# Earlier routes and two sets of early tiles in a sketched-attention and expert kernel

## The chip, the cores and the metric

The kernel runs on one core of one Trainium2 chip. The metric is the time of one execution in device microseconds. The kernel before took 250.34 us, the median of three runs (250.05 to 256.19). The profile shows one execution, of 226.58 us by the same measure, with a span of 224.9 us from its first to its last instruction; all times inside the kernel below are of that span.

The engines have these names in the profile: PE is TensorE (matmuls and transposes), DVE VectorE, ACT ScalarE, POOL GpSimd, and SP SyncE, which does no arithmetic and issues transfers. Each works through its own instructions in order, and semaphores tie them together.

## What is computed

Two blocks follow each other. The first is attention without a softmax: each query and key of 32 numbers becomes 64 products of two sketches, and the sum over a sequence is then a small matrix for each head.

```python
phi(x) = outer(S1 @ x, S2 @ x)            # 8 x 8 = 64 numbers
kv = einsum('bhsf,bhsd->bhfd', phi(k), v); z = sum(phi(k), axis=s)
x = (phi(q) @ kv) / (phi(q) @ z + 1e-6)   # batch 4, heads 4, 1088 tokens, head size 32
```

The result, 4352 tokens of 128 numbers, goes into the second block, a layer of eight experts in which every token goes to one of them:

```python
e = argmax(x @ w_gate); gate = softmax(x @ w_gate)[e]
out = gate * sigmoid(x @ w_output_gate)[e] * (relu(x @ w1[e]) @ w2[e])   # 128 -> 1024 -> 128
```

All numbers are float32 on the chip.

## The kernel before, in words

**Chunks and groups.** The 4352 tokens are 34 chunks of 128. Four chunks make a group, so there are nine groups, the last of two chunks. The arrays lie in memory turned, so that a group of keys or queries is one transfer.

**Attention stages.** Each group of keys goes through ks (sketch on PE), kb (copy on ACT), kp (products on DVE, L362) and kc (sums on PE, L405, which collect the matrix of a batch; a batch ends inside a chunk). cl, gt, gs, gm and gc close a batch and fold the gate weights into its matrix, so that the attention matmul yields the gate logits too. Each group of queries goes through qs, qb, qp (L362), qt and qc (transposes on PE, L416, and their copy on ACT), qa (the attention matmul on PE, L430), qr, qx (L447, L448), ql (L456) and qz (L463). Queries of a batch need that batch closed.

**Routes.** ROUTES (line 42) joins groups into routes. When the logits of a route are there, rc chooses the expert of each token (L488 to L500), rg and rf make the gate factor, rp counts the tokens ahead of each one by two matmuls (L516, L517), rs makes the row numbers, and rd (send, L538) scatters each chunk of the route by an indirect transfer of GpSimd (L544) into the table xs in memory. There, each expert has its own region, filled from its front; a row holds the 128 numbers, the factor, and the token's number. A counter, carry, runs from route to route. After the last route a last scatter (L796) writes padding behind each expert's rows.

**Tiles.** A tile is 128 rows of one expert. Its stages are tx (transpose of the rows, PE, L803), tv (copy, DVE, L808), tu (8 blocks of the first expert matrix, PE, L815), th (relu, ACT, L822), td (the second matrix, PE, L829), ty (factor, ACT, L839) and to (scatter to the output by GpSimd, L844). The rows of a tile are read by rows(t) (L632), and its two halves of weights, 512 KB each, by weights(t, 0) and weights(t, 1) (L639). Both are issued by SP, at an address from a table that DVE makes (eti: experts, bti: first rows). There are three weight buffers (NW = 3). weights(t + 3, 0) stands behind tu(t), weights(t + 3, 1) behind td(t), and each waits until PE has read the buffer that it overwrites. A load is left out when the buffer has that expert already.

**Early tiles.** When a route is counted but not the last, every expert has some rows already, and its full groups of 128 can be taken as tiles at once. With E = 8 experts at most 8 x 127 rows are not in full groups, so after 16 chunks (MARK = 1, the second route) at least NE = 9 tiles are full (line 232). mn counts, mt calls early_tiles (L584) for their table, then issues weights of tiles 0 to 2 and the rows of all nine. After the last route late_tiles (L595) makes the table of the rest, of which there are NT - NE at most.

**Order of the work.** PLAN (line 32) is an order written out by hand: attention, routes, and the first tiles, stage by stage. Stages are emitted in just this order, and every engine gets its part of it in this order. The loads of keys and queries follow it too, as far as their buffers (NK, NV, NQ) have room. After PLAN, step_(t) takes the tiles in a regular way: tx(t + 2), tv(t + 2), tu(t + 1), th(t + 1), td(t), ty(t), to(t). In td(t) (L825), behind the weights, rows(t + NX) is issued; with NX = 5 that is five tiles ahead, and when t + 3 is 8, the rows of tiles 9 and 10 are issued together. Scatters into xs are declared free of each other (group "rows"), and those of routes behind the mark are declared free of the loads of early rows (group "early"), since they touch other rows.

**Rings.** Row buffers (xin) number NE + NX + 2 = 16, output buffers (y) NE + 1 = 10.

Of the kernel before, what the change touches and what calls it, by code (L numbers as in the profile page):

```python
# [13 lines left out]
F32 = mybir.dt.float32  # L14
I32 = mybir.dt.int32
ALU = mybir.AluOpType
# [3 lines left out]
EPS = 1e-6  # L20
GRP = 512
WARM = 6
NK, NV, NQ = 4, 5, 2
TS = 128
NW = 3
NX = 5

PLAN = """
    ks0 kb0 ks1 kp0 kb1 ks2 kp1 kc0 kb2 kc1 kp2 qs0 kc2 ks3 qb0 cl0 qp0 gt0 kb3 kc2 gs0 kp3 bg0 qt0 qs1 qc0 gm0 qb1
    qs2 gc0 qp1 qa0 qb2 qp2 ks4 qr0 qx0 qt1 kb4 ql0 ks5 kp4 qc1 kc3 kb5 qz0 qs3 kp5 kc4 qb3 qa1 cl1 qp3 kc4 qr1 qx1
    gt1 qt3 gs1 ql1 gm1 qz1 qc3 ks6 rc0 gc1 ks8 kb6 qa3 kb8 kp6 rg0 rp0 qr3 qt2 rs0 rf0 qs4 qc2 qx3 rd0 kc5 qb4 ql3
    qp4 kc6 qa2 cl2 qz3 gt2 qr2 kp8 qt4 gs2 qx2 gm2 qc4 qs5 ql2 qz2 gc2 ks7 rc1 qb5 qa4 kb7 qp5 rp1 rg1 kc6 qr4 rs1
    qt5 rf1 mn1 kp7 qs7 qc5 rd1 mt1 qb7 kc7 kc8 qs6 qx4 qb6 ql4 qp6 qa5 cl3 qp7 gt3 qr5 qt6 gs3 qx5 gm3 qc6 qs8 ql5
    qz4 gc3 qt7 qb8 qz5 rc2 qa6 qc7 qa7 qr6 qp8 rg2 qx6 rp2 qr7 ql6 qx7 qt8 ql7 qc8 tx0 rs2 tx1 qa8 tv0 tv1 rf2 tx2
    qr8 tu0 tv2 rd2 qx8 ql8 qz8 tx3 th0 tu1 tv3 qz7 qz6 rc3 tx4 th1 td0 tv4 rg3 rp3 tu2 ty0 rs3 rf3 rc4 td1 th2 rg4
    mn4 tu3 mt4 ty1 rd3 td2 th3 tu4 ty2 rf4 rp4 th4 tx5 rs4 tx6 td3 tv5 tv6 rd4 mp4  # L40
"""
ROUTES = ((0, 1), (2, 3), (4, 5), (6,), (7, 8))
MARK = 1
NOWHERE = 1 << 20


# [5 lines left out]
def kernel(  # L52
# [12 lines left out]
    nc = tc.nc  # L65
# [3 lines left out]
    DM = H * D  # L69
    E = w_d.shape[0]  # L70
# [8 lines left out]
    W = DM + 16  # L79
    CAP = N + TS  # L80
    NT = (N + E * (TS - 1)) // TS
    PR = E * TS // 128

    consts = ctx.enter_context(tc.tile_pool(name="consts", bufs=1))
# [10 lines left out]
    def ring(pool, tag, n, shape):  # L95
        turns[tag] = [pool.tile(shape, F32, tag=f"{tag}{i}", name=f"{tag}{i}") for i in range(n)], [0]
# [89 lines left out]
    def half(a):  # L186
        return slice(a * FC * 128, (a + 1) * FC * 128)
# [21 lines left out]
    ones = consts.tile([128, 128], F32, tag="ones")  # L209
# [15 lines left out]

    routes = [range(groups[r[0]][0], groups[r[-1]][-1] + 1) for r in ROUTES]
    duo = {g: i for i, r in enumerate(ROUTES) for g in r}
    RG = max(len(rs) for rs in routes)

    NE = -(-((routes[MARK][-1] + 1) * 128 - E * (TS - 1)) // TS)
    assert 0 < NE <= NT
    ring(consts, "xsT", 3, [128, TS])
    ring(consts, "hT", 2, [128, FC, TS])
    ring(consts, "y", NE + 1, [TS, DM])
    ring(consts, "xin", NE + NX + 2, [TS, W])
    eps = consts.tile([128, 1], F32, tag="eps")
    nc.gpsimd.memset(eps, EPS)
    fresh = {}  # L240
# [15 lines left out]
    pad = consts.tile([128, PR, W], F32, tag="pad")  # L256
# [19 lines left out]
    stepT = consts.tile([128, NT], F32, tag="stepT")  # L276
# [261 lines left out]
    def send(i, ey, sloti, co):  # L538
        n = len(routes[i])
        x = xts.pop(i)  # L540
        nc.gpsimd.tensor_copy(x.bitcast(I32)[:, :n, DM + 1], ids[:, routes[i][0]:routes[i][-1] + 1])
        nc.gpsimd.tensor_mul(x[:, :n, DM], co[:, :n], ey[:, :n, E + 1])  # L542
        for j in range(n):
            apart("rows", nc.gpsimd.indirect_dma_start(  # L544
                out=xs[:, :], out_offset=bass.IndirectOffsetOnAxis(ap=sloti[:, j:j + 1], axis=0),
                in_=x[:, j], in_offset=None, bounds_check=E * CAP - 1), *(["early"] if i > MARK else []))


    eti = consts.tile([128, NT], I32, tag="eti")
    bti = consts.tile([128, NT], I32, tag="bti")  # L550

    def spread(t, n):
        return t[:, :E].unsqueeze(1).to_broadcast((128, n, E))

    def table(t0, n, ends, jump, first, last=None):


        past = consts.tile([128, n, E], F32, tag=f"past{t0}", name="past")
        et = consts.tile([128, n], F32, tag=f"et{t0}", name="et")
        nc.vector.tensor_tensor(past, step[:, :n].unsqueeze(2).to_broadcast((128, n, E)), spread(ends, n), op=ALU.is_ge)  # L560
        with nc.allow_low_precision("numbers of experts are whole"):
            nc.vector.tensor_reduce(eti[:, t0:t0 + n], past[:, :, :E - 1], axis=AX, op=ALU.add)
        nc.vector.tensor_mul(past, past, spread(jump, n))
        nc.vector.tensor_reduce(et, past[:, :, :E - 1], axis=AX, op=ALU.add)
        if last is None:
            nc.vector.tensor_tensor(bti[:, t0:t0 + n], et, stepT[:, :n], op=ALU.add)
        else:

            nc.vector.scalar_tensor_tensor(out=et, in0=et, scalar=first, in1=stepT[:, :n], op0=ALU.add, op1=ALU.add)
            nc.vector.tensor_scalar(bti[:, t0:t0 + n], et, last, None, op0=ALU.min)  # L570

    NS = N // TS
    more = consts.tile([128, 1], I32, tag="more")
    done = consts.tile([128, E + 1], F32, tag="done")
    nc.vector.memset(done, 0.0)
    early = consts.tile([128, E + 1], F32, tag="early")
    nc.vector.memset(early, 0.0)

    def counted():
        ps = psum.tile([128, E], F32, tag="rt", name="ps_n")  # L580
        nc.tensor.matmul(ps, ones, state["carry"], start=True, stop=True)
        return ps

    def early_tiles(ps):  # L584
        full = consts.tile([128, E], I32, tag="full")
        jump = consts.tile([128, E], F32, tag="jump")
        nc.vector.tensor_tensor(full, ps, ecap, op=ALU.subtract)
        nc.vector.tensor_single_scalar(full, full, TS.bit_length() - 1, op=ALU.logical_shift_right)
        nc.vector.tensor_tensor_scan(done[:, 1:], ones[:, :E], full, 0.0, op0=ALU.mult, op1=ALU.add)
        nc.vector.tensor_scalar_min(done[:, 1:], done[:, 1:], float(NE))  # L590
        nc.vector.tensor_sub(early[:, :E], done[:, 1:], done[:, :E])
        nc.vector.tensor_scalar(jump, early[:, :E], -float(TS), float(CAP), op0=ALU.mult, op1=ALU.add)
        table(0, NE, done[:, 1:], jump, None)

    def late_tiles(ps):  # L595
        num = consts.tile([128, E], F32, tag="num")
# [17 lines left out]
        nc.vector.tensor_tensor_scan(ends, ones[:, :E], nt, 0.0, op0=ALU.mult, op1=ALU.add)  # L614
        nc.vector.tensor_single_scalar(more, ends[:, E - 1:], float(NS - NE), op=ALU.subtract)
        nc.vector.tensor_tensor(jump, early[:, 1:], left, op=ALU.subtract)
# [6 lines left out]
    regs, xin, xTs, hTs = {}, {}, {}, {}  # L623
# [5 lines left out]
    def rows(t):  # L629
        at = value(bti, t, E * CAP - TS)  # L630
        xin[t] = nxt("xin")
        ins = nc.sync.dma_start(xin[t], xs[bass.ds(at, TS), :])  # L632
        if t < NE:
            tc.add_to_no_dep_group("early", ins.ins)

    def weights(t, a):
        if a == 0:
            regs[t] = value(eti, t, E - 1)
        nc.sync.dma_start(wt[t % NW][a].rearrange("p c x -> p (c x)"),  # L639
                          w_d[bass.ds(regs[t], 1), :, half(a)].rearrange("e p x -> p (e x)"),  # L640
                          cond=regs[t] != regs[t - NW] if t >= NW else None)
# [12 lines left out]
    stages, have, did = {}, {}, set()  # L654
    end = [NT]
# [123 lines left out]

    @stage  # L780
    def mt(i):
        if i == MARK:
            early_tiles(have.pop(("mn", i)))
            for t in range(NW):
                weights(t, 0)
                weights(t, 1)
            for t in range(NE):
                rows(t)
        else:
            late_tiles(have.pop(("mn", i)))  # L790

    @stage
    def mp(i):
        pa, pai = have.pop("pai")
        nc.gpsimd.tensor_copy(pai, pa)
        apart("rows", nc.gpsimd.indirect_dma_start(  # L796
            out=xs[:, :], out_offset=bass.IndirectOffsetOnAxis(ap=pai[:, :1], axis=0),
            in_=pad.rearrange("p a b -> p (a b)"), in_offset=None), "early")

    @stage  # L800
    def tx(t):
# [22 lines left out]
    @stage  # L824
    def td(t):  # L825
        hT = have.pop(("th", t))
        ps = have["td", t] = nxt("kvz").rearrange("p a x -> p (a x)")[:, :DM]
        for c in range(FC):
            nc.tensor.matmul(ps, hT[:, c], wt[t % NW][1][:, c], start=(c == 0), stop=(c == FC - 1))  # L829
        if t + NW < end[0]:  # L830
            weights(t + NW, 1)
        if t + NW >= NE - 1:
            for n in range(NE if t + NW == NE - 1 else t + NX, min(t + NX + 1, end[0])):
                rows(n)

    @stage
    def ty(t):
# [85 lines left out]
```

## Time and profile before

| what | value |
|---|---|
| time, median of three runs | 250.34 us |
| span of the profiled execution | 224.9 us |
| mean granted clock of PE | 0.958 |
| PE busy, DVE, ACT, POOL | 200.6, 69.3, 74.0, 78.8 us |
| bytes moved, mean rate | 49.10 MB, 218 GB/s |
| scatters L544, first and last start | 35.0 and 90.6 us |
| first tile half (L815), start in the timeline | 65.1 us |
| last second half (L829), start | 213.2 us |

The page has several parts. The slices divide the span into 40 equal pieces of 5.6 us and give the busy share of each engine in tenths; PEclk is the clock that PE was granted, in tenths of full speed. The waits list who waited for whom, in us in total, times, and longest. The chain is followed back from the last instruction, at each step to what released it. The timeline gives instructions in order of time: start, duration, engine, line, operation, tiles, count, and in square brackets the idle time ahead of it and what ended it. "DMA to landing" is the time from the issue of a transfer to its completion.

### The profile page before, as it was taken

The numbers are of one execution on the slowest core, as the hardware profiler recorded it, in microseconds if no ns is written. First come the engines' busy times: TensorE is split into PE (matmuls) and PEld (weight loads), VectorE is DVE, ScalarE is ACT, GpSimd is POOL, SyncE is SP. The second block draws the span as 40 slices with busy tenths as digits, with TensorE's granted clock in tenths as the row PEclk, the third lists the DMA queues.
The fourth block names the chain that finished last, engine by engine and source line by source line (L and its number), as shares of the span: only waits on it lengthen the run. The fifth ranks groups of instructions, "written<-read, shape, count | busy, mean of one in ns | idle before, by whom it ended". The sixth has DMA issues, their size and how long they took to land.

```text
span 224.9 us, 6588 instructions
## 1 busy us (share of the span) xinstructions
PE 200.6 (89%) x2458; PEld 194.9 (87%) x2458; DVE 69.3 (31%) x221; ACT 74.0 (33%) x140; POOL 78.8 (35%) x130
## 2 busy tenths in 40 slices
PE   7899999999489999907999999999999999999720
PEld 6889999998379999907999999999999999999720
DVE  4557889999645670000000010101010101010000
ACT  2123343425204343400434343433434343434300
POOL 3700006777037747771131313132222223131310
PEclk9999999999958999995999999999999999999995
DMA  5866512349636989966898789989984686883100
GB/s 160 315 193 225 155 50 77 115 117 357 247 94 175 319 294 282 312 254 197 251 315 322 227 237 319 313 314 312 330 311 143 207 263 189 269 292 114 38 30 1
DMA packets 21634, 49.10 MB, mean 218 GB/s; under 512 B 3466, under 2 KB 9100, under 8 KB 21600
## 3 DMA queue, kind: packets, MB, share of 16 engines
q1 hardware_dynamic: 19024, 43.31, 60.2%
q0 software_dynamic: 2416, 5.33, 6.3%
q8 instruction: 21, 0.34, 0.7%
q14 instruction: 13, 0.11, 0.2%
q10 hardware_dynamic: 160, 0.01, 0.0%
HBM read 51.17 MB, written 5.52 MB: 252 GB/s over the span
## 4 chain that ended last, share of the span: by engine, by line
PE 56%; DMA 22%; issue 9%; POOL 7%; DVE 1%; SPq 0%; POOLq 0%; ACT 0%
PE w L815 22%; PE kvz L829 18%; DMA out_dram<-y,xin 12%; POOL xs L544 7%; PE t L346 5%; DMA xs<-pad,pai 4%; PE w L430 2%; PE kvz L405 2%; DMA xs<-x,sloti 2%; DMA wt<-in_w_dram 2%; DMA xin<-xs 2%; PE t L803 2%; PE w L322 2%; PE w L416 1%; DVE kp L362 1%
## 5 line engine op out<-in xcount | busy, mean ns | idle before, releaser
L815 PE MATMUL w<-xsT,wt 128*128 128x128 f32 x592 | 76.0, 284 | 0.0
L829 PE MATMUL kvz<-wt,hT 128*128 128x128 f32 x592 | 72.5, 276 | 1.5 <-SPq L875 1.5
L815 PEld LDWEIGHTS w<-xsT,wt 128*128 128x128 f32 x592 | 72.8, 201 | 0.0
L829 PEld LDWEIGHTS kvz<-wt,hT 128*128 128x128 f32 x592 | 69.5, 193 | 1.7 <-issue 1.7
L844 POOL DMA_INDIRECT out_dram<-y,xin x37 | 35.9, 970 | 88.1 <-DMA wt<-in_w_dram 46.4
L822 ACT ACTIVATE hT<-w 128x1024 f32<-128x1024 f32 x37 | 37.9, 1023 | 69.2 <-PE w L815 69.2
L808 DVE COPY xsT<-t 128x128 f32<-128x128 f32 x38 | 11.0, 291 | 121.9 <-PE t L803 121.9
L544 POOL DMA_INDIRECT xs<-x,sloti x34 | 33.7, 990 | 12.2 <-issue 8.8
L839 ACT ACTIVATE y<-kvz,xin 128x128 f32<-128x128 f32 x37 | 13.6, 367 | 28.6 <-PE kvz L829 28.6
L803 PE MATMUL t<-ident,xin 128*128 128x128 f32 x38 | 11.0, 295 | 10.3 <-DMA xin<-xs 10.3
L803 PEld LDWEIGHTS t<-ident,xin 128*128 128x128 f32 x38 | 5.6, 150 | 11.1 <-DMA xin<-xs 10.9
L430 PE MATMUL w<-kz,qpT 128*64 128x98 f32 x272 | 13.8, 256 | 0.4 <-ACT b_sb L354 0.4
L430 PEld LDWEIGHTS w<-kz,qpT 128*64 128x64 f32 x272 | 12.4, 142 | 0.9 <-ACT b_sb L354 0.5
L542 POOL TENSOR_TENSOR x<-co,ey 128x8 f32<-128x8 f32 (+2 forms) x5 | 1.1, 223 | 33.5 <-DVE rc L447 23.7
L422 ACT COPY qpT<-w 128x1024 f32<-128x1024 f32 (+1 forms) x9 | 8.7, 965 | 9.9 <-PE w L416 9.9
L362 DVE TENSOR_TENSOR qp<-t,b_sb 128x1024 f32<-128x1024 f32 (+1 forms) x9 | 10.4, 1160 | 3.0 <-ACT b_sb L354 2.8
L362 DVE TENSOR_TENSOR kp<-t,b_sb 128x1024 f32<-128x1024 f32 (+1 forms) x9 | 10.4, 1160 | 2.9 <-PE kvz L405 1.8
L405 PE MATMUL kvz<-vt,kp 128*64 128x65 f32 (+1 forms) x288 | 10.5, 223 | 0.0
L346 PE MATMUL t<-Sb,kT 128*64 128x64 f32 x272 | 9.8, 224 | 0.8 <-DVE kp L362 0.5
L354 ACT COPY b_sb<-t 128x128 f32<-128x128 f32 (+1 forms) x18 | 4.7, 259 | 16.4 <-PE t L346 16.1
L346 PEld LDWEIGHTS t<-Sb,kT 128*64 128x64 f32 x272 | 8.7, 138 | 1.6 <-DVE kp L362 0.6
L405 PEld LDWEIGHTS kvz<-vt,kp 128*64 128x64 f32 (+1 forms) x288 | 9.4, 137 | 0.5 <-issue 0.2
(130 smaller groups left out, 120.8 us busy)
## 6 DMA issues: line engine op xcount, KB each, us to landing
wt<-in_w_dram SPq DMA_DIRECT2D x79, 512.0 KB
xin<-xs SPq DMA_DIRECT2D x41, 72.0 KB
vt<-in_v_dram SPq DMA_DIRECT2D x8, 260.0 KB
kT<-in_k_dram SPq DMA_DIRECT2D x8, 256.0 KB
qT<-in_q_dram SPq DMA_DIRECT2D x8, 256.0 KB
out_dram<-y,xin POOLq DMA_INDIRECT x37, 4.7
xs<-x,sloti POOLq DMA_INDIRECT x34, 4.4
vt<-in_v_dram SPq DMA_DIRECT2D x1, 130.0 KB
```

The source lines that it names most:

```text
L346: nc.tensor.matmul(ps[64 * t:64 * (t + 1), j * H:(j + 1) * H], src[:, j * 128 + 64 * t:j * 128 + 64 * (t + 1)], Sb[i], start=i == 0 and j ...
L362: nc.vector.tensor_mul(res[:, :n], bview(av, [list(av.ap[1]), list(av.ap[2]), [0, r]]), bview(bv, [list(bv.ap[1]), [0, r], list(bv.ap[2])]))
L405: nc.tensor.matmul(acc[b][64 * h:64 * (h + 1), s], kp[p0:p0 + np_, j * H + 2 * s + h].rearrange("s i j -> s (i j)"), vt[p0:p0 + np_, j, s] ...
L430: nc.tensor.matmul(ps[64 * t:64 * (t + 1), 2 * j + s, :VG], qpT[:, 2 * j + s, 64 * t:64 * (t + 1)], kz[(c * 128 + 64 * t) // S][:, s], sta ...
L544: apart("rows", nc.gpsimd.indirect_dma_start(out=xs[:, :], out_offset=bass.IndirectOffsetOnAxis(ap=sloti[:, j:j + 1], axis=0), in_=x[:, j] ...
L803: nc.tensor.transpose(have["tx", t], xin[t][:, :DM], ident)
L808: nc.vector.tensor_copy(have["tv", t], have.pop(("tx", t)))
L815: nc.tensor.matmul(ps[:, c], wt[t % NW][0][:, c], xT, start=True, stop=True)
L822: nc.scalar.activation(have["th", t], have.pop(("tu", t)), ACTF.Relu)
L829: nc.tensor.matmul(ps, hT[:, c], wt[t % NW][1][:, c], start=(c == 0), stop=(c == FC - 1))
L839: nc.scalar.activation(have["ty", t], have.pop(("td", t)), ACTF.Copy, scale=xin[t][:, DM:DM + 1])
L844: apart("out", nc.gpsimd.indirect_dma_start(out=out, out_offset=bass.IndirectOffsetOnAxis(ap=x.bitcast(I32)[:, DM + 1:DM + 2], axis=0), in ...
```

## The change

The routes become 4, 8, 8, 8 and 6 chunks, and there are two marks in place of one: tiles 0 to 4 are full behind 12 chunks (the second route), tiles 5 to 12 behind 20 chunks (the third). early_tiles runs once at each mark and takes the full groups that are new since the mark before. The aim is to have rows for the first tiles sooner, and more of them ahead of the late rows, which wait for the last route and the padding. Scatters are declared free of the loads of the early tiles of every mark that lies before them.

PLAN is written anew: first queries come ahead of later keys, and some transposes of tiles stand further ahead. Query buffers become three, NX becomes 4, the ring of row buffers 20 and that of output buffers 14. At the first mark the rows of tiles 0 to 4 are issued, each behind its weights; all other rows, t + NX from tile 5 on, are issued one by one in td(t).

```diff
-NK, NV, NQ = 4, 5, 2
+NK, NV, NQ = 4, 5, 3
-NX = 5
+NX = 4
-ROUTES = ((0, 1), (2, 3), (4, 5), (6,), (7, 8))
-MARK = 1
+ROUTES = ((0,), (1, 2), (3, 4), (5, 6), (7, 8))
+MARKS = (1, 2)
-    NE = -(-((routes[MARK][-1] + 1) * 128 - E * (TS - 1)) // TS)
+    NES = [-(-((routes[m][-1] + 1) * 128 - E * (TS - 1)) // TS) for m in MARKS]
+    NE = NES[-1]
-    ring(consts, "y", NE + 1, [TS, DM])
-    ring(consts, "xin", NE + NX + 2, [TS, W])
+    ring(consts, "y", 14, [TS, DM])
+    ring(consts, "xin", 20, [TS, W])
 ...
-                in_=x[:, j], in_offset=None, bounds_check=E * CAP - 1), *(["early"] if i > MARK else []))
+                in_=x[:, j], in_offset=None, bounds_check=E * CAP - 1), *(f"early{k}" for k, m in enumerate(MARKS) if i > m))
 ...
-    def early_tiles(ps):
+    def early_tiles(k, ps):
+        t0, t1 = ([0] + NES)[k:k + 2]
+        was, now = earlies[k:k + 2]
 ...
+        nc.vector.tensor_tensor(new, full, was[:, :E], op=ALU.subtract)
+        nc.vector.tensor_tensor_scan(ends[:, 1:], ones[:, :E], new, 0.0, op0=ALU.mult, op1=ALU.add)
+        nc.vector.tensor_scalar_min(ends[:, 1:], ends[:, 1:], float(t1 - t0))
+        nc.vector.tensor_sub(new, ends[:, 1:], ends[:, :E])
+        nc.vector.tensor_add(now[:, :E], was[:, :E], new)
 ...
+        table(t0, t1 - t0, ends[:, 1:], jump, first)
 ...
-        if t < NE:
-            tc.add_to_no_dep_group("early", ins.ins)
+        for k, n in enumerate(NES):
+            if t < n:
+                tc.add_to_no_dep_group(f"early{k}", ins.ins)
 ...
-        if i == MARK:
-            early_tiles(have.pop(("mn", i)))
-            for t in range(NW):
-                weights(t, 0)
-                weights(t, 1)
-            for t in range(NE):
+        if i in MARKS:
+            early_tiles(MARKS.index(i), have.pop(("mn", i)))
+        if i == MARKS[0]:
+            for t in range(NES[0]):
+                if t < NW:
+                    weights(t, 0)
+                    weights(t, 1)
                 rows(t)
 ...
-        if t + NW >= NE - 1:
-            for n in range(NE if t + NW == NE - 1 else t + NX, min(t + NX + 1, end[0])):
-                rows(n)
+        if NES[0] <= t + NX < end[0]:
+            rows(t + NX)
```

The new PLAN, in the part that matters for the first tiles (route 3 is sent by rd3, route 4 by rd4):

```
tx0 qr7 qa5 tv0 qx7 ql7 mn2 tx1 qr5 tx2 tv1 tu0 qx5 ql5 tv2 tx3 qz7 th0 tu1 tv3 mt2 td0 th1 tu2 qz5 ty0 rc3 td1
th2 qz8 rg3 to0 rp3 ty1 tx4 rs3 tu3 to1 tv4 rc4 td2 th3 rf3 rg4 tu4 rd3 ty2 rf4 td3 th4 rp4 ty3 tx5 tx6 tv5 td4
rs4 tv6 tu5 ty4 tx7 th5 tx8 tv7 tu6 tv8 td5 th6 to4 tx9 ty5 tu7 tv9 rd4 td6 th7 tx10 ty6 mn4 tu8 mt4 td7 th8
tx11 ty7 tu9 tv11 tv10 to6 td8 th9 mp4
```

More of the change, by code (lines that the diff above doesn't have):

```diff
@@ L22 @@
 WARM = 6
-NK, NV, NQ = 4, 5, 2
+NK, NV, NQ = 4, 5, 3
 TS = 128
 NW = 3
-NX = 5
+NX = 4
 PLAN = """
[L33 to L40, printed above, removed]
-"""
-ROUTES = ((0, 1), (2, 3), (4, 5), (6,), (7, 8))
-MARK = 1
+    ks0 kb0 ks1 kp0 kb1 ks2 kp1 kc0 kb2 qs0 kp2 kc1 qb0 qp0 ks3 kc2 ks4 kb3 cl0 bg0 kp3 gt0 kb4 qt0 gs0 qs1 qc0 gm0
+    qb1 kc2 gc0 qp1 qa0 kp4 qt1 qr0 qx0 qs2 qc1 ql0 ks5 qz0 qb2 rc0 kc3 kb5 kc4 qa1 qp2 rg0 cl1 rp0 qr1 kp5 qt2 ks6
+    rs0 qc2 qx1 gt1 qs3 ql1 gs1 kb6 qz1 gm1 qb3 rf0 kc4 gc1 qp3 rd0 qa2 kp6 qt3 qr2 qx2 ks7 qc3 ql2 kc5 qz2 kb7 rc1
+    kc6 qa3 cl2 rp1 rg1 kp7 kc6 qr3 ks8 rs1 kc7 kb8 rf1 gt2 kp8 rd1 qs4 gs2 qx3 gm2 qb4 ql3 kc8 gc2 qp4 qs8 mn1 qb8
+    cl3 qt4 qp8 mt1 qt8 qc4 qs6 qc8 qa4 qb6 qp6 gt3 qr4 qs7 gs3 qx4 gm3 qb7 qt6 ql4 gc3 qp7 qa8 qc6 qs5 qz4 qr8 qz3
+    qt7 qb5 qx8 ql8 qp5 qc7 qa6 rc2 qt5 qr6 qc5 qx6 rp2 rg2 ql6 rs2 qa7 rf2 qz6 rd2 tx0 qr7 qa5 tv0 qx7 ql7 mn2 tx1
+    qr5 tx2 tv1 tu0 qx5 ql5 tv2 tx3 qz7 th0 tu1 tv3 mt2 td0 th1 tu2 qz5 ty0 rc3 td1 th2 qz8 rg3 to0 rp3 ty1 tx4 rs3
+    tu3 to1 tv4 rc4 td2 th3 rf3 rg4 tu4 rd3 ty2 rf4 td3 th4 rp4 ty3 tx5 tx6 tv5 td4 rs4 tv6 tu5 ty4 tx7 th5 tx8 tv7
+    tu6 tv8 td5 th6 to4 tx9 ty5 tu7 tv9 rd4 td6 th7 tx10 ty6 mn4 tu8 mt4 td7 th8 tx11 ty7 tu9 tv11 tv10 to6 td8 th9
+    mp4
+"""
+ROUTES = ((0,), (1, 2), (3, 4), (5, 6), (7, 8))
+MARKS = (1, 2)
 NOWHERE = 1 << 20
@@ L228 @@
     RG = max(len(rs) for rs in routes)
-    NE = -(-((routes[MARK][-1] + 1) * 128 - E * (TS - 1)) // TS)
-    assert 0 < NE <= NT
+    NES = [-(-((routes[m][-1] + 1) * 128 - E * (TS - 1)) // TS) for m in MARKS]
+    NE = NES[-1]
+    assert 0 < NES[0] and NE <= NT
     ring(consts, "xsT", 3, [128, TS])
     ring(consts, "hT", 2, [128, FC, TS])
-    ring(consts, "y", NE + 1, [TS, DM])
-    ring(consts, "xin", NE + NX + 2, [TS, W])
+    ring(consts, "y", 14, [TS, DM])
+    ring(consts, "xin", 20, [TS, W])
     eps = consts.tile([128, 1], F32, tag="eps")
@@ L565, in table @@
         if last is None:
-            nc.vector.tensor_tensor(bti[:, t0:t0 + n], et, stepT[:, :n], op=ALU.add)
+            nc.vector.scalar_tensor_tensor(out=bti[:, t0:t0 + n], in0=et, scalar=first, in1=stepT[:, :n],
+                                           op0=ALU.add, op1=ALU.add)
         else:
@@ L573 @@
     more = consts.tile([128, 1], I32, tag="more")
[L574 to L577, printed above, removed]
+    earlies = [consts.tile([128, E + 1], F32, tag=f"early{k}", name=f"early{k}") for k in range(len(MARKS) + 1)]
+    for x in earlies:
+        nc.gpsimd.memset(x, 0.0)
+    early = earlies[-1]
     def counted():
@@ L582, in counted @@
         return ps
-    def early_tiles(ps):
-        full = consts.tile([128, E], I32, tag="full")
-        jump = consts.tile([128, E], F32, tag="jump")
+    def early_tiles(k, ps):
+        t0, t1 = ([0] + NES)[k:k + 2]
+        was, now = earlies[k:k + 2]
+        full = consts.tile([128, E], I32, tag=f"full{k}", name="full")
+        new = consts.tile([128, E], F32, tag=f"new{k}", name="new")
+        ends = consts.tile([128, E + 1], F32, tag=f"ends{k}", name="ends")
+        jump = consts.tile([128, E], F32, tag=f"jump{k}", name="jump")
+        first = consts.tile([128, 1], F32, tag=f"first{k}", name="first")
         nc.vector.tensor_tensor(full, ps, ecap, op=ALU.subtract)
+        nc.vector.memset(ends[:, :1], 0.0)
         nc.vector.tensor_single_scalar(full, full, TS.bit_length() - 1, op=ALU.logical_shift_right)
[L589 to L593, printed above, removed]
+        nc.vector.tensor_tensor(new, full, was[:, :E], op=ALU.subtract)
[3 more added lines that the diff above has]
+        nc.vector.tensor_add(now[:, :E], was[:, :E], new)
+        nc.vector.tensor_tensor(jump, was[:, 1:], now[:, :E], op=ALU.subtract)
+        nc.vector.tensor_scalar(jump, jump, float(TS), float(CAP), op0=ALU.mult, op1=ALU.add)
+        nc.vector.tensor_scalar_mul(first, was[:, :1], float(TS))
+        table(t0, t1 - t0, ends[:, 1:], jump, first)
     def late_tiles(ps):
@@ L781, in mt @@
     def mt(i):
-        if i == MARK:
-            early_tiles(have.pop(("mn", i)))
-            for t in range(NW):
-                weights(t, 0)
-                weights(t, 1)
-            for t in range(NE):
+        if i in MARKS:
[5 more added lines that the diff above has]
+                    weights(t, 1)
                 rows(t)
-        else:
+        elif i not in MARKS:
             late_tiles(have.pop(("mn", i)))
@@ L797, in mp @@
             out=xs[:, :], out_offset=bass.IndirectOffsetOnAxis(ap=pai[:, :1], axis=0),
-            in_=pad.rearrange("p a b -> p (a b)"), in_offset=None), "early")
+            in_=pad.rearrange("p a b -> p (a b)"), in_offset=None), *(f"early{k}" for k in range(len(MARKS))))
     @stage
```

## The prediction

> **What bounds the kernel now.** I read the page first (busy shares and slices), then TensorE's waits, the chain that ended last, and the order of time around the two holes. TensorE (PE) is busy 89% of the span; the slices show where it is not: slices 10 and 11, and 17 and 18 (counted from 0).
>
> ```profile
> PE 200.6 (89%) x2458; PEld 194.9 (87%) x2458; DVE 69.3 (31%) x221; ACT 74.0 (33%) x140; POOL 78.8 (35%) x130
> PE   7899999999489999907999999999999999999720
> PEclk9999999999958999995999999999999999999995
> ```
>
> PE's waits say what the holes are: the transposes of token rows (L803) stand for rows read back from the table in memory.
>
> ```profile
> PE t L803 <- DMA xin<-xs: 10.3, 3, 6.8
> PE kvz L829 <- SPq L875: 1.5, 1, 1.5
> ```
>
> The chain (start, us, what) gives the way into each: the last scatter of the marked route lands at 60.15 and its rows are read; later the pad scatter lands at 100.7, then the first late rows.
>
> ```profile
> 54.87 5.26 DMA xs<-x,sloti
> ...
> 60.99 1.90 DMA xin<-xs
> ...
> 92.06 8.63 DMA xs<-pad,pai
> 100.71 1.89 DMA xin<-xs
> ```
>
> PE's timeline after the second hole shows a second price: the first two halves of a tile take 3.62 and 2.24 us where 1.95 is usual, because the clock was granted at half.
>
> ```profile
> 102.64 0.48 PE L803 MATMUL t<-ident,xin 128*128 128x128 f32 x1 [6.80 <-DMA xin<-xs]
> 102.91 3.62 PE L815 MATMUL w<-xsT,wt 128*128 128x128 f32 x16
> 106.33 2.24 PE L829 MATMUL kvz<-wt,hT 128*128 128x128 f32 x16
> 108.41 0.27 PE L803 MATMUL t<-ident,xin 128*128 128x128 f32 x1
> 108.52 1.95 PE L815 MATMUL w<-xsT,wt 128*128 128x128 f32 x16
> ```
>
> Elsewhere PE runs one tile per 3.68 us without a wait (starts of L803 3.68 apart). This stretch of the timeline shows the order SyncE (SP) keeps: a tile's second half ends near 138.0, SP at once issues the weights into the freed buffer, and 0.9 us later the rows of a later tile.
>
> ```profile
> 137.87 0.27 PE L803 MATMUL t<-ident,xin 128*128 128x128 f32 x1
> ...
> 138.06 0.33 SPq L639 DMA_DIRECT2D wt<-in_w_dram  x1
> ...
> 138.97 0.33 SPq L632 DMA_DIRECT2D xin<-xs  x1
> ...
> 141.55 0.27 PE L803 MATMUL t<-ident,xin 128*128 128x128 f32 x1
> ...
> 145.23 0.27 PE L803 MATMUL t<-ident,xin 128*128 128x128 f32 x1
> ```
>
> Rows issued at 138.97 are those of the transpose at 145.23 (NX = 5): a lead of 6.3 us. What they need, by the tile's own view:
>
> ```profile
> DMA to landing us min/median/max: 2.2/4.7/5.6
> ```
>
> So this prefetch has 0.7 us to spare at its worst. By windows the landing is 2.3 with no weights ahead of it (at 100.7), and 3.8 to 5.6 behind a loaded weight half.
>
> **What the Trainium skill says.** "TensorE: Matmul & The Clock Gate", section "Why this matters for your kernels": no idle gaps over about 3 us, or the clock falls back. The trace agrees: after the 2.93 us hole (with 0.53 on each side) and after the 6.80 us hole the granted clock was 0.5 for a time. Same page, "Step-by-step: what each phase is for": matmuls stay in program order, so a transpose whose rows are missing holds everything behind it; the 6.8 us hole is one such. "DMA: Bandwidth & Descriptors", "Anatomy of one DMA": a fixed 2.0 us for each transfer, and semaphores are waited for at the issuing sequencer; the trace has 2.2 as its least landing, and SP's queue standing 7.7 us for the pad.
>
> **Part by part.** *Removed: the two holes.* First: 0.53 + 2.93 + 0.53 = 4.0 idle, and cold excess: chain pieces of L815 3.41 and 2.06 against 1.79, plus some 0.2 at L430 and the transposes, 2.1. Second: 6.8 idle and (3.41 - 1.79) + (2.04 - 1.79) + 0.2 = 2.1. Together 15.0. Rows of tiles 0 to 4 now need 12 chunks: their scatters end a route sooner, and the late rows have four more tiles ahead of them (4 x 3.68 = 14.7 us against a hole of 6.8). I take PE's first tile half at 65.3 - 4.0 = 61.3.
>
> *Attention reordered.* The same products, transposes and matmuls; DVE and PE were both nearly full up to 59 us (DVE 9.4 of 10 us in 50 to 60). The second early_tiles and five more small operations in each: 16 x 0.2 + 5 x 0.2 = 4.2 us of DVE, of which about one lies before the first tile and three beside the tile stage, where DVE is idle most of the time. Fewer L-sums, logits and route work before the first tile give about 2 back. Zero, with plus or minus 2 for the range.
>
> *Weights.* The routing worked out from the inputs gives 37 tiles in both kernels; a tile reloads its buffer unless the tile three before has the same expert, 32 loads before and 34 after. Two more megabytes beside PE work: zero.
>
> *NX 5 to 4, rows issued one by one.* Before, rows 0 to 8 are issued together. Now only 0 to 4 are; rows t + 4 are issued in td(t), behind the weights that wait for td(t). In the built order of instructions the next transposes stand like this:
>
> - Tile 6: rows leave after td2, transpose after tu4, td3 and a placement (4.2 us later). Need 1.0 + 4.7 = 5.7: wait 1.3 (bounds 0 to 1.5).
> - Tile 7: here a new wait comes in. In the built program this load waits for the last scatter of the fourth route (chunks 20 to 27): those scatters were declared free of the early loads, but the load, which now comes later in the program, is not free of them. Placement 3 ends near 61.3 + 5 x 1.79 + 0.5 = 70.7; slots 0.44, a copy 0.2, the choice for six chunks 1.75 and factor 0.57 on DVE follow (73.6); first scatter 0.95 later (as 64.31 to 65.26), seven more at 1.28 (83.5), landing 4.4 (median of xs): 87.9. The rows then land in 2.3 with an empty queue: 90.3. PE is at this transpose after eleven halves: 61.3 + 19.7 + 1.9 + 1.3 = 84.2. Wait 6.1 (bounds 3 to 8). Queued behind it on SP: weights of tile 7 and rows 8; on PE everything.
> - Tile 8: rows issued at about 89.4, landing 3.8: 93.2, PE there at 90.4: 2.8 (1.8 to 3.7).
> - Tiles 9, 10, 11: the transpose stands directly behind td5, td6, td7, whose end releases the weights ahead of the rows. Wait = 1.0 from the end of td to the row issue + landing. I take 3.8, the least landing measured behind a loaded half, as the queue is emptier than before: 4.8 x 3 = 14.4 (3.3 x 3 = 9.9 to 5.7 x 3 = 17.1). Tile 10's wait for the fifth route's scatters is over by then.
> - From tile 12 on the lead is one step less the issue: 2.7 us against 3.8. A wait lengthens the lead of the next, so per tile s = 1.0 + 3.8 - 3.68 - s, s = 0.56. For 23 of 25 tiles a load stands ahead (worked out from the inputs): 12.9 (landing 2.7: 0; 4.7: 23). Pad and late rows are in time, since PE comes later.
>
> *Clock.* Four holes of 2.8 to 6.1 us, shaped like the two that went cold: three drops at 2.1, 6.3 (0 to four full ones, 13.6).
>
> Sum: 1.3 + 6.1 + 2.8 + 14.4 + 12.9 + 6.3 = 43.8 added, 15.0 removed: +28.8. Span 224.9 + 28.8 = 253.7; time 250.34 + 28.8 = 279.1 (the timed runs lie 23.8 above the profiled 226.58; I carry this over).
>
> **Rivals.** *A, the holes close and the rows are in time:* 250.34 - 15.0 = 235.3. For it: the scatters do get earlier, and PE is the bound. Against it: tiles 9 to 11 have a negative lead in the order of instructions; no landing in the trace is under 2.2. *B, waits at their least:* 0 + 3 + 1.8 + 9.9 + 0 = 14.7 against 15.0: 250.0, no change. For it: landings of 2.3 exist where weights are not reloaded. Against it: nearly all tiles reload. *C, the DMA engines stay as full as in steady state (0.9 busy) and the clock stays cold through tiles 7 to 11:* 1.5 + 8 + 3.7 + 17.1 + 13.6 + 23 + 2 for a late first tile = 68.9 - 15.0: 304.2. For it: landings of 4.8 to 5.6 were usual between 130 and 160 us, with all weights reloaded. Against it: longer steps thin out the traffic.
>
> **How the numbers follow.** Main case 0.72, A 0.06, B 0.08, C 0.14. Time 279.1. Range 256 to 300: A and B lie below, a part of C above. Faster 0.06, within 2% 0.07, slower 0.87 (B split over the bound).
>
> **What would show it.** PE's waits with L821 (the same transpose) on xin as the longest by far, near 37 us over some 28 waits; SP's queue waiting once on xs for several us near 80; holes directly after the second halves of tiles 5, 6, 7; a step of about 4.2 in place of 3.68 later; the clock at half near 85 to 120; and the first tile near 61 with no hole at tile 13. Wrong if steps stay at 3.68 (landings under 2.7), or if transposes of tiles 9 to 11 don't wait.

## The result, and the profile after

The changed kernel takes 295.12 us (median of four runs, 293.9 to 296.65), beside 251.59 for the kernel before (250.05 to 256.19): a ratio of 1.176, 95% interval 1.163 to 1.188. It is slower by 43.5 us, where 28.8 were forecast. The time lies in the forecast range.

One thing is needed to read the numbers below: the kernel before takes 253.8 us on one of four chips that the later runs met and 225 us on the three others, and the profile that the prediction was read from (span 224.9) is of the shorter kind, while the time on record is of the longer. So each time below stands beside that of the kernel before on the same chip. Each chip was met on one occasion only; whether the chip or the occasion decides is open, and "kind of chip" says no more than which of the two times the kernel before takes there.

From the page of the changed kernel, from the runs on record (span 294.5 us): busy time of TensorE (PE), its 40 slices and the granted clock. Then PE's longest wait: us in total, times, longest.

```profile
PE 223.2 (76%) x2460; PEld 210.5 (71%) x2460; DVE 72.0 (24%) x240; ACT 73.7 (25%) x140; POOL 79.3 (27%) x133
PE   7799988398739953584488798877978798879840
PEclk9999998579988995756879989999979979999995
```

```profile
PE t L821 <- DMA xin<-xs: 41.8, 23, 5.4
```

The slices hardly reach 9 after the twentieth, and one wait stands for it: the transpose of token rows (L821, L803 before) waits for rows read back, 41.8 us in 23 times where the profile of the kernel before had 10.3 in three. Of the 41.8 us, tiles 6 to 11 have 22.4 and the later ones 19.4.

This profile is not of the same kind of chip as the profile before. The same program on a chip where the kernel before takes 225.28 us took 277.51 (ratio 1.232, 1.225 to 1.238), with a span of 275.3 us. That trace can be laid beside the one of before line by line, and all that follows on single waits is from it. Its slices and clock (PE busy 215.8 us in all), and PE's longest wait:

```profile
PE   7889999983998835728599669888979898879930
PEclk9999999999599768786689999999999999999995
```

```profile
PE t L821 <- DMA xin<-xs: 43.2, 27, 5.2
```

The timeline of PE at the first tiles (start, us, what, and in brackets the idle time ahead of it). Before, the first tile half (L815, now L833) stood here:

```profile
65.11 3.62 PE L815 MATMUL w<-xsT,wt 128*128 128x128 f32 x16
```

Now:

```profile
61.44 0.33 PE L821 MATMUL t<-ident,xin 128*128 128x128 f32 x1
64.11 0.33 PE L821 MATMUL t<-ident,xin 128*128 128x128 f32 x1 [0.52 <-DMA xin<-xs]
68.30 0.45 PE L821 MATMUL t<-ident,xin 128*128 128x128 f32 x1 [3.86 <-DMA xin<-xs]
68.54 3.64 PE L833 MATMUL w<-xsT,wt 128*128 128x128 f32 x16
```

The hole ahead of the tiles is still there, 0.52 + 3.86 us, and the first tile half begins 3.4 us later than before, not 4.0 sooner. The chain of waits (start, us, what) says why:

```profile
51.34 4.68 DMA xs<-x,sloti
56.04 0.33 SPq L647
...
56.88 1.04 SPq L655
...
58.96 0.33 SPq L647
...
59.79 0.33 SPq L655
...
61.19 6.98 DMA xin<-xs
```

SyncE (SP) issues weights (L655) and rows (L647) by turns. The rows of tile 0 wait for the last scatter of their routes (landed at 56.02), and the weights of tiles 1 and 2, which need no scatter, stand behind them in SP's queue; the rows of tiles 1 to 4 stand behind those. The last link, the landing of rows behind these weights, lasts 6.98 us, where the least landing of rows in this trace is 2.2. On the longer kind of chip the hole does not appear: there the first tile half begins at 76.71, and no transpose of tiles 0 to 3 waits for rows.

Tiles 9 and 10, in the timeline of PE of the same trace (at tile 11 the same: 4.44 us of waiting, then a half of 3.62):

```profile
111.89 0.45 PE L821 MATMUL t<-ident,xin 128*128 128x128 f32 x1 [4.81 <-DMA xin<-xs]
112.13 3.46 PE L833 MATMUL w<-xsT,wt 128*128 128x128 f32 x16
115.43 1.95 PE L847 MATMUL kvz<-wt,hT 128*128 128x128 f32 x16
122.55 0.45 PE L821 MATMUL t<-ident,xin 128*128 128x128 f32 x1 [5.17 <-DMA xin<-xs]
123.08 3.76 PE L833 MATMUL w<-xsT,wt 128*128 128x128 f32 x16
```

Each transpose comes straight after a second half (L847), whose end lets the weights and then its rows go; after each of these three holes the matmuls run at half clock (granted 0.50; 3.46 to 3.76 us instead of 1.95). And the steady stage, in PE's timeline:

```profile
182.28 0.33 PE L821 MATMUL t<-ident,xin 128*128 128x128 f32 x1 [0.99 <-DMA xin<-xs]
...
184.24 1.95 PE L847 MATMUL kvz<-wt,hT 128*128 128x128 f32 x16
...
186.54 0.33 PE L821 MATMUL t<-ident,xin 128*128 128x128 f32 x1 [0.35 <-DMA xin<-xs]
...
191.34 0.33 PE L821 MATMUL t<-ident,xin 128*128 128x128 f32 x1 [0.90 <-DMA xin<-xs]
```

Transposes are 4.26 and 4.80 us apart instead of 3.68; from tile 12 on, 25 steps (144.89 to 258.09), the mean step is 4.53.

### The profile page after: what moved, and what is told of

It reads as the page before. It is cut to its first block, busy times and chain, and to the rows that moved or that the text cites. A ratio compares the mean times of both kernels' runs of the same rounds, so it can differ in the third digit from the quotient of the medians.

```text
span 294.5 us, 6603 instructions
## 1 busy us (share of the span) xinstructions
PE 223.2 (76%) x2460; PEld 210.5 (71%) x2460; DVE 72.0 (24%) x240; ACT 73.7 (25%) x140; POOL 79.3 (27%) x133
## 4 chain that ended last, share of the span: by engine, by line
issue 32%; PE 27%; DMA 17%; POOL 8%; another core or an unknown queue 7%; DVE 3%; POOLq 1%; ACT 1%; SPq 1%; DVEq 0%
DMA out_dram<-y,xin 11%; POOL out_dram L861 7%; PE t L349 6%; PE w L833 5%; PE kvz L847 4%; PE kvz L408 4%; PE w L433 3%; DMA xin<-xs 3%; DMA wt<-in_w_dram 3%; PE w L419 2%; PE w L325 1%; DVE qp L365 1%; POOL xs L547 1%; DMA xs<-x,sloti 1%
## 5 line engine op out<-in xcount | busy, mean ns | idle before, releaser
L833 PE MATMUL w<-xsT,wt 128*128 128x128 f32 x592 | 82.5, 299 | 0.9 <-issue 0.9
L847 PE MATMUL kvz<-wt,hT 128*128 128x128 f32 x592 | 77.1, 286 | 5.9 <-ACT hT L840 4.5
L833 PEld LDWEIGHTS w<-xsT,wt 128*128 128x128 f32 x592 | 78.8, 214 | 1.1 <-issue 1.1
L847 PEld LDWEIGHTS kvz<-wt,hT 128*128 128x128 f32 x592 | 74.4, 204 | 6.3 <-ACT hT L840 4.7
L821 PE MATMUL t<-ident,xin 128*128 128x128 f32 x38 | 12.3, 328 | 42.7 <-DMA xin<-xs 41.8
L821 PEld LDWEIGHTS t<-ident,xin 128*128 128x128 f32 x38 | 5.7, 151 | 47.4 <-DMA xin<-xs 28.7
L419 PE MATMUL w<-ident,qp 128*128 128x128 f32 x68 | 11.2, 307 | 4.9 <-DVE qp L365 4.7
L349 PE MATMUL t<-Sb,kT 128*64 128x64 f32 x272 | 10.9, 225 | 3.7 <-issue 2.7
L419 PEld LDWEIGHTS w<-ident,qp 128*128 128x128 f32 x68 | 8.3, 155 | 6.5 <-DVE qp L365 5.1
L349 PE MATMUL t<-Sb,qT 128*64 128x64 f32 x272 | 11.5, 236 | 1.1 <-issue 1.1
L349 PEld LDWEIGHTS t<-Sb,qT 128*64 128x64 f32 x272 | 10.0, 148 | 2.8 <-issue 2.7
```

The source lines that it names most:

```text
L349: nc.tensor.matmul(ps[64 * t:64 * (t + 1), j * H:(j + 1) * H], src[:, j * 128 + 64 * t:j * 128 + 64 * (t + 1)], Sb[i], start=i == 0 and j ...
L419: nc.tensor.transpose(ps[:, 2 * j + s], qp[:, j * H + 2 * s:j * H + 2 * s + 2].rearrange("p h i j -> p (h i j)"), ident)
L821: nc.tensor.transpose(have["tx", t], xin[t][:, :DM], ident)
L833: nc.tensor.matmul(ps[:, c], wt[t % NW][0][:, c], xT, start=True, stop=True)
```

## The experiments

*The kernel before, unchanged,* to see what its longer executions look like.

> The kernel before, unchanged. It is run again because its profile (226.6 us) and its timed runs (250 to 256) lie 24 us apart, while the changed kernel's profile (296.3) and timed runs agree. If the 24 us are stretches in which TensorE and those that wait for it stand while GpSimd issues scatters (seen in the changed kernel at 49 to 57 and 78 to 86 us), a profile near 250 shows such stretches before 95 us and the same tile stage after it. If they are spread over the whole span (a slower clock, slower transfers), the tile step after 105 us is longer than 3.68. Time: 250 either way.

253.31 us beside 253.81 (ratio 1.000, 0.998 to 1.003), span 251.2. From PE's waits and timeline:

```profile
PE t L803 <- DMA xin<-xs: 1.0, 1, 1.0
```

```profile
82.21 1.95 PE L815 MATMUL w<-xsT,wt 128*128 128x128 f32 x16
```

Its waits for rows are 1.0 us in all, not 10.3: PE loses the time elsewhere, 17.1 us of it before the first tile half (82.21 against 65.11), and the tile stage after it steps by 3.68 again. So on this chip nearly nothing of the waits for rows that the prediction took off was there to be taken.

*The changed kernel with only the row lead put back.*

```
-NX = 4
+NX = 5
```

> The changed kernel with NX = 5: rows of every tile from 5 on are issued one tile sooner, nothing else. Theory 1 (rows come too late for their transposes, 22.4 us at tiles 6 to 11, 19.4 later, 13.5 of cold clock): most of these 55 us go, 236 to 250 us, steps of 3.68. Theory 2 (the new order of attention and routes is what costs: the first tile came at 76.7 and not at 61): 280 to 295. Theory 3 (the DMA engines are too full, two more weight loads and more traffic at once): the waits turn from xin to wt, 275 to 295.

256.69 us beside 253.81 (1.010, 1.006 to 1.014). From the waits of PE:

```profile
PE t L821 <- DMA xin<-xs: 4.9, 2, 3.4
PE w L419 <- DVE qp L365: 4.8, 1, 4.8
```

One step of lead takes 36.9 of the 41.8 us of waiting away, and 38.4 us of time: against 295.12 on record, and against 295.13 on the same chip for the kernel of the next experiment but one, which keeps the shorter lead. The expectation that most of the waiting goes came true; its 236 to 250 us did not. What is left of the change gained nothing here.

*The kernel before with only the row lead taken.*

```
-NX = 5
+NX = 4
```

> The kernel before with NX = 4, nothing else: the nine early rows are still issued together, only the rows of later tiles come one tile later. Theory 1: waits at the transposes of tiles 10 on, some 0.8 us a tile as in the changed kernel (19.4 over 25 tiles) and a few cold stretches: 265 to 278. Theories 2 and 3: 248 to 253.

279.95 us (1.101, 1.090 to 1.112), just above the 265 to 278 expected. From PE's waits:

```profile
PE t L803 <- DMA xin<-xs: 22.1, 15, 2.7
```

The shorter lead alone, with the old routes and order, costs 26 us. The rest of the 41 I put down to the early tiles, argued and not tried: the kernel before issues rows 0 to 8 together, so no transpose meets its rows' issue there.

*The changed kernel with the early rows also free of later scatters,* which takes away SP's wait ahead of tile 7.

```
+            for k, m in enumerate(MARKS):
+                if i > m:
+                    tc.add_to_no_dep_group(f"late{k}", ins.ins)
 ...
+            tc.declare_no_dep(ins.ins, group=f"late{k}", reason="the rows are distinct")
```

> The changed kernel, NX = 4 kept, with the loads of early rows declared free of the scatters of routes behind their mark, so that tile 7's rows don't wait for the fourth route nor tile 10's for the fifth. Theory 1: SyncE's wait of 5.7 us on xs goes, the transposes of tiles 7 and 8 wait less, those of 9 to 11 as before: 287 to 293. Theory 2: 294 to 296, no change.

295.13 us, where 287 to 293 were expected if that wait costs time: no gain against the 295.12 on record. From the waits of PE:

```profile
PE t L828 <- DMA xin<-xs: 41.8, 24, 5.6
```

The sum is that of the changed kernel to the tenth, in one wait more. Tile 7 waited 3.62 us in the profile on record and now doesn't wait at all; tiles 8, 9 and 10 wait longer by 1.5, 1.2 and 0.8. So what tile 7 saved, the next ones paid, and SP's wait for the scatters did not set the time.

*Do the scatters hold TensorE?* In the longer executions PE stands while GpSimd issues scatters (last section). Two kernels replace them by plain transfers to fixed rows, in the kernel before; one does so in the changed kernel. They leave out the placing of rows by expert, so their tiles hold other tokens; the scatters of padding and of results stay.

```
-            apart("rows", nc.gpsimd.indirect_dma_start(
-                out=xs[:, :], out_offset=bass.IndirectOffsetOnAxis(ap=sloti[:, j:j + 1], axis=0), ...
+                e, k = FIXED[c]
+                ins = nc.gpsimd.dma_start(xs[e * CAP + k * TS:e * CAP + (k + 1) * TS, :], x[:, j] ...)
```

> The kernel before, in which GpSimd writes each chunk's 128 rows to 128 fixed neighbouring rows of xs with a plain transfer, in place of the indirect scatter of line 544 (left out: the placing by expert, so the tiles hold other tokens; three more transfers fill the places that the chunks leave, so the tile count and every other instruction stay). Theory S, the indirect scatters hold TensorE while GpSimd issues them: without them the time falls from 253 to 224-238 us, since the profile of before that stood at 226.6 us had none of this standing. Theory S', whatever transfer GpSimd issues holds TensorE: 246-254. Theory N, the standing has another cause and only lies beside the scatters: 249-255, and matmuls in groups of 4 to 6 behind waits marked issue near 38 and 60 us all the same.

> As the kernel with plain transfers from GpSimd, but SyncE issues them, so GpSimd issues no transfer before the tiles (left out: the placing of rows by expert, as there). Theories S and S' (GpSimd's issuing holds TensorE): 224-236 us, and the holes of about 10 us at the first tiles' transposes come back, since the attention half ends some 20 us sooner. Theory N: 249-255.

> The changed kernel with the same edit: SyncE writes fixed rows with plain transfers in place of the indirect scatters (left out: the placing of rows by expert). If the holding by the scatters is what my sum missed, this kernel lands where the sum put the changed one: 268-282 us against 295. If the missing 15 us lie elsewhere (larger waits for rows, a colder clock), it stays at 290-297.

These three met a chip where the kernel before took 225.3 us. There the plain transfers from GpSimd gave 223.93 (0.995, 0.988 to 1.002), those from SyncE 228.3 (1.011, 1.004 to 1.018): no standing to take away, so these two do not tell the theories apart. The changed kernel with plain transfers took 272.03, with 45.3 us of waits for rows. That it lands inside 268 to 282 is no proof of the expectation's reason: beside 225.3 it is 46.7 slower. Most of the loss is there without the scatters of rows (with them it is 52.2 beside such a kernel before, as the next experiment shows), so the missing microseconds of my sum had to be looked for in the tiles. The kernel before with SyncE's transfers, on another chip:

> The kernel before with plain transfers of fixed rows from SyncE in place of the indirect scatters (left out: the placing of rows by expert), once more. If the kernel before takes 253 us here, theory S (the scatters hold TensorE): 226-236 and no matmuls in groups of 4 to 6 behind waits marked issue at 38 and 60 us; theory N (another cause): 250-257 with these groups. If the kernel before takes 225 us: 227-229 as in the last comparison, no news.

227.94 beside 225.28 (1.012, 1.007 to 1.018): no standing here either, and no news.

*The changed kernel itself on the shorter kind of chip.*

> The changed kernel once more, beside the kernel before. If the kernel before takes 225 us here as in the last comparison: the sum of the prediction (+28.8) gives 254; theory A, it held but for the holes that are missing in longer executions: 252-258; theory B, the waits for rows and the colder clock are larger than the sum had them, whatever the standing at the scatters does: 266-273 (as with plain transfers, 272), with some 40-45 us of waits for rows. If the kernel before takes 253 us: 294-297 as before, no news.

277.51 beside 225.28. Theory A (252 to 258) is out: not the missing holes alone, but the sum's own terms were too small. 277.5 overshoots theory B's 273 too; its 40 to 45 us of waits for rows came true (43.2).

*Weights ahead of rows at the first mark.*

```
-            for t in range(NES[0]):
-                if t < NW:
-                    weights(t, 0)
-                    weights(t, 1)
-                rows(t)
+            for t in range(NW):
+                weights(t, 0)
+                weights(t, 1)
+            for t in range(NES[0]):
+                rows(t)
```

> The changed kernel with one line group moved: at the first mark all six weight loads are issued before the five row loads, as the kernel before does, in place of weights and rows by turns. Theory H (the rows of tile 0 wait for the scatters of the second route, and the weights and rows of tiles 1 and 2 queue behind them, which is why the hole ahead of the first tile half stayed): the transposes of tiles 1 and 2 wait under 1 us instead of 0.5 and 3.9, the first tile half comes 3.5-5 us sooner, and the time falls by 4-7 us: 270-274 beside 277.5 where the kernel before takes 225 us, or 289-293 beside 295 where it takes 253. Rival (rows come late by the scatters' own landing, not by the queue): no change, 276-279 or 294-297.

272.73 us beside 225.06 (1.207, 1.197 to 1.217). PE's timeline at the first tiles:

```profile
62.34 0.33 PE L821 MATMUL t<-ident,xin 128*128 128x128 f32 x1 [1.49 <-DMA xin<-xs]
...
64.60 1.95 PE L833 MATMUL w<-xsT,wt 128*128 128x128 f32 x16
```

The first tile half begins 3.9 us sooner and at full clock, and the time falls by 4.8 us from the 277.51 of another chip of this kind. Theory H holds, though 1.49 us of waiting stay, more than the "under 1" expected: the last scatter lands at 57.12, and the rows take 5.16 us behind six halves of weights. Not all that is gained lasts: the small matmuls that count the fifth route come 6.7 us sooner (81.30 instead of 88.02), the last second half only 4.1, as tile 6 now waits longer.

*Rows further ahead,* first with the later rows six ahead, then with the weights in front and the later rows five ahead. Both also put the scatter of padding ahead of second half 7.

```
-        if NES[0] <= t + NX < end[0]:
-            rows(t + NX)
+        for n in range(NES[0], end[0]):
+            if n not in asked and n <= t + (NXE if n < NE else NX):
+                asked.add(n)
+                rows(n)
```

> The changed kernel with rows issued further ahead, at no other cost: 8 tiles ahead for the 13 early tiles, 6 for the later ones (NX = 6), and the pad's scatter moved ahead of second half 7. Theory 1, the issue of rows is what costs: the waits for rows of 4.9 us that NX = 5 left go, with about 1 us of clock: 247-251 us, just under the kernel before (253). Rival: the waits for rows are gone at NX = 5 but for a little, and what is left is held by the attention half: 253-257.

> The changed kernel with the rows of the 13 early tiles issued up to 8 tiles ahead, later ones 5 (NX = 5), weights first at the first mark, the pad's scatter ahead of second half 7. Expected from the trace with NX = 6 (227.9 us beside 225.3): minus the 5.0 us wait for weights behind the rows of tile 13 and about 3 us of cold clock after it, minus 4-6 us at the first tiles: 214-220 us beside 225 for the kernel before, or 243-249 beside 253. Rival: the attention half or another wait fills what is freed: 224-228, or 252-256.

The first (NX = 6, NXE = 8) took 227.92 beside 225.3 (1.008, 1.000 to 1.016): not under the kernel before, as expected, but 49.6 us under the changed kernel's 277.5 on another chip of this kind, nearly all of the 52.2. Its waits for rows are 2.9 us in the profiled execution (230.17, the longest of four). What PE waits for there instead, and SP's timeline:

```profile
PE w L834 <- DMA wt<-in_w_dram: 5.0, 1, 5.0
```

```profile
94.57 0.33 SPq L648 DMA_DIRECT2D xin<-xs  x1
...
97.53 12.83 SPq L656 DMA_DIRECT2D wt<-in_w_dram  x7
```

The rows issued at 94.57 are those of tile 11, eight ahead: they wait in SP's queue for the last scatter of the fourth route, the weights of tile 8 (97.53) stand behind them, and PE waits 5.0 us for these. The expectation of the second kernel took them for the rows of tile 13, which are issued only at 110.94; so its smaller NX could not take this wait away by the reason it gave.

The second (NX = 5, NXE = 8) took 224.50 beside 225.06: a ratio of 0.996, 0.994 to 0.999. Its waits of PE:

```profile
PE kvz L848 <- DMA wt<-in_w_dram: 4.7, 1, 4.7
PE t L822 <- DMA xin<-xs: 1.6, 1, 1.6
```

The rival came true: 224 to 228, not 214 to 220. The rows of tile 5 wait on SP for the third route's scatters until 76.7, and weights of tiles 4 and 5 stand behind them; that is the wait of 4.7 us. The wait for the weights of tile 8 is still there, with 1.3. One wait took the place of another. So the new routes and order, with rows in time, are worth about half a microsecond on this chip.

## Why the prediction was right, and where its sum was not

The direction, and the reason for it, hold: the shorter lead for rows makes the kernel slower. It was shown from both sides: given back, it takes away 38 of 41 us (of 295.1 - 253.8); taken from the kernel before, it costs 26. The forecast time, 279.1, was 16 below the 295.1 measured, and that it came so near is in part luck, as two errors of opposite sign stand in it. Beside a kernel before of 225.3 us the change costs 52.2, 23.4 more than the sum. On record, beside 251.59, it costs 43.5, 8.7 less than that: the changed kernel loses 17.6 us to the longer kind of chip (277.5 to 295.1) where the kernel before loses 26.3 (225.3 to 251.6), and the prediction carried its 23.8 us over as if both lost the same. The waits for rows that it took off were hardly there on the longer kind, but on the shorter, where they are, the sum fell short too: the span is longer by 50.4 us (275.3 - 224.9) instead of 28.8. Term by term, on that pair of traces:

| term of the sum | predicted, us | measured, us |
|---|---|---|
| first hole closes | -4.0 | +3.4 (first tile half 68.54 against 65.11) |
| cold clock after it | -2.1 | +0.6 (3.64 + 2.98 against 3.62 + 2.26, and 0.2 in before's later halves) |
| second hole closes, with its clock | -8.9 | -8.8 |
| tiles 6, 7, 8 | 1.3 + 6.1 + 2.8 = 10.2 | 1.86 + 2.25 + 2.73 = 6.8 |
| tiles 9 to 11 | 14.4 | 4.81 + 5.17 + 4.44 = 14.4 |
| steady state | 12.9 | 17.6 |
| clock | 6.3 | 10.0 (excess over 1.95 in eight halves of tiles 4 to 9) |
| emptied pipeline | none | 6.2 (what is left) |
| sum | +28.8 | +50.3 (last second half 263.49 against 213.20) |

*Removed: the two holes* failed for the first one, and this was the largest miss (10.1 us with its clock). The step took the rows of tiles 0 to 4 for free once their scatters end a route sooner. It overlooked an edit that is in the diff: weights and rows by turns on one queue. The Trainium skill, "DMA: Bandwidth & Descriptors", section "Anatomy of one DMA", says that semaphores are waited for at the issuing sequencer; the prediction used this for tile 7 and not here, where the trace shows it (weights of tile 1 issued at 56.88, those of tile 0 at 49.94). The experiment with weights first shows it for 3.9 us of the late start and for the cold clock (6.7 us together at the count of the fifth route). Even so its first half begins at 64.60 instead of the 61.3 predicted: 1.49 us are still waited for rows, and about 2 us are lost in the attention part (below). The second hole closed as forecast.

*Tile 7* had the mechanism, not the size. The first scatter of the fourth route leaves at 85.08, not 74.5, because the first tile half was late and the plan puts the route's steps between tile halves; the rows left at 96.44. But PE was late as well, and waited 2.25 us, not 6.1. That taking SP's wait away gained nothing on the longer kind of chip says that the term was worth about zero there.

*Tiles 9 to 11* are right to the tenth in their sum: rows of tile 9 leave 0.9 us after the second half (107.09 to 107.97), and those of tiles 9 and 10 land in 3.79 and 3.73 (3.8 taken). Single waits lie up to 0.4 beside the 4.8 taken for each, and cancel out.

*Steady state.* The alternation was foreseen: 0.91, 0, 2.21, 0, 2.30, 0 at tiles 12 to 17, then small waits at most tiles. The sum is 17.6 instead of 12.9: over the 23 tiles of the sum 0.77 each instead of 0.56. The landing is the term mis-sized: 3.8 was taken, and over all rows it is 4.5 at the median. Put into the prediction's own sum, 4.5 gives 0.91 a tile, 20.9 in all, so the measured sum lies between the two.

*Emptied pipeline* was in no step. Where nothing is waited for, 16 matmuls are followed by the next after 1.79 us (158.54 to 160.33), though the view lists 1.95 for them. At 184.24 a second half starts and ends by the view at 186.19, the transpose waits 0.35 and starts at 186.54: it could have started at 184.24 + 1.79 = 186.03, and itself delays the next half by 0.17 (to 186.71) instead of 0.11. A wait of 0.35 thus costs 0.57, some 0.22 more than is listed. As an estimate from this place, 25 waits make 5.5 of the 6.2 left; no run tried it.

*Clock.* Three drops were taken, "shaped like the two that went cold". In fact eight halves of tiles 4 to 9 ran slow, from 2.58 to 3.76 us. The Trainium skill, "TensorE: Matmul & The Clock Gate", section "Why this matters for your kernels", speaks of gaps over about 3 us. The trace agrees for the longer ones: each of 4.4 to 5.2 us was followed by a half of 3.46 to 3.76. Below that the length doesn't decide: at 154.69 and 164.58, after 2.21 and 2.30 us, the next half took 1.96 and 1.95, while at tile 6, after a wait of 1.86 us with only small matmuls and a transpose in the 0.7 us ahead of it, the next two took 3.00 and 2.58. What decides there stays open.

*Attention reordered* at nothing, with 2 us either way for the range, holds only at the edge of that range on the shorter kind of chip. Ahead of the first tile PE has a wait there that the kernel before lacks:

```profile
59.94 1.58 PE L433 MATMUL w<-kz,qpT 128*64 128x98 f32 x32 [1.35 <-DVE t L526]
```

L526 is VectorE's work on the row numbers of the third route, which the new order puts among the last queries. Without its 1.49 us for rows, the kernel with weights first would start its first half near 63.1, some 2 us after the 61.1 (65.11 - 4.0) that the kernel before would have without its own. On the longer kind the new order starts the tiles 5.5 us sooner instead (76.71 against 82.21). In the end, with rows in time, the changed kernel is within about 1% of the one before on both kinds. *Weights* at nothing: no run sets them apart. The end of the tiles has no new wait but the 1.6 us that was there before (1.5).

## What to carry to other kernels

A prefetch distance is to be counted in the written order of the issuing queue, from the instruction that lets the transfer go to the one that needs it; where both stand side by side, the whole landing shows. In this kernel each hole cost more than the wait listed (an estimated 0.2 us of pipeline, and half clock after the longer ones). A load that must wait for something has no place between loads that need not, as all that stand behind it on its queue wait too. And a gain read from one profile is first to be found again in the executions whose time is to be forecast.

## What the runs showed that was not expected

The kernel before takes 28 us longer on one chip than on three others, and the traces show where PE stands. With 253 us, while GpSimd issues scatters (POOL, L544), PE gets on by five matmuls at a time, and an engine that waits for PE goes on only after the last scatter (here issued at 44.38). Timeline of the unchanged kernel before, span 251.2 us:

```profile
38.78 0.46 PE L430 MATMUL w<-kz,qpT 128*64 128x98 f32 x5 [0.30 <-issue]
39.27 0.97 POOL L544 DMA_INDIRECT xs<-x,sloti  x1 [0.30 <-issue]
...
39.54 0.46 PE L430 MATMUL w<-kz,qpT 128*64 128x98 f32 x5 [0.30 <-issue]
...
46.91 0.27 ACT L436 ACTIVATE rc<-w,eps 128x16 f32<-128x16 f32 x1 [11.67 <-remote]
```

With 225 us the same scatters (35.03 to 45) lie beside the same matmuls, all 32 in one piece, and ACT follows PE at once:

```profile
36.26 1.58 PE L430 MATMUL w<-kz,qpT 128*64 128x98 f32 x32
...
37.89 0.27 ACT L436 ACTIVATE rc<-w,eps 128x16 f32<-128x16 f32 x1 [2.79 <-PE w L430]
```

That the scatters cause the standing was not shown: the kernels without them ran where it doesn't occur. What differs between the chips, or between the occasions, stays open.
